# Staging slots from spent load slots, and two key gradient blocks moved behind dq, in a decode step with its gradients

## The chip, the cores and the metric

The kernel runs on one core of a Trainium2 chip. The metric is the device time of one execution in microseconds (us). The profile is of one execution on the same core; its engines are PE (TensorE matmul), PEld (TensorE weight load), DVE (VectorE), ACT (ScalarE), POOL (GpSimd) and SP (SyncE, which issues loads).

## What is computed

The reference is two rounds of a block pair, on one token for each of two batch rows, and the gradient of everything with respect to a given output gradient:

```python
def _A_ref(x, k_cache, v_cache, wq, wo):            # 32 query heads, 4 key/value heads, Sk = 16384, Dh = 128
    q = (x @ wq).reshape(B, Sq, Hq, Dh).transpose(0, 2, 1, 3)
    k, v = jnp.repeat(k_cache, rep, axis=1), jnp.repeat(v_cache, rep, axis=1)
    p = _softmax(jnp.einsum("bhqd,bhkd->bhqk", q, k) * (Dh ** -0.5), axis=-1)
    o = jnp.einsum("bhqk,bhkd->bhqd", p, v)
    return o.transpose(0, 2, 1, 3).reshape(B, Sq, Hq * Dh) @ wo

def _B_ref(x, w1, b1, w2, b2):                      # 1024 -> 3584 -> 1024
    return jnp.einsum("bsf,fd->bsd", _gelu(jnp.einsum("bsd,df->bsf", _layernorm(x), w1) + b1), w2) + b2

x = A_x
x = x + _A_ref(_layernorm(x), A_k_cache, A_v_cache, A_wq, A_wo)
x = x + _B_ref(_layernorm(x), B_w1, B_b1, B_w2, B_b2)
x = x + _A_ref(_layernorm(x), A_k_cache, A_v_cache, A_wq, A_wo)   # the same weights and caches again
x = x + _B_ref(_layernorm(x), B_w1, B_b1, B_w2, B_b2)
# returned: x, and the gradients of A_x, A_k_cache, A_v_cache, A_wq, A_wo, B_w1, B_b1, B_w2, B_b2
```

All tensors are bfloat16. The key cache, the value cache and their two gradients have 32 MB each; they are most of the 450 MB that are moved.

## The kernel before

**Order of work.** The kernel first records a list of small pieces of work (`emit`), each with the pieces of SBUF (`Chunk`) that it uses, and then `Program.run` plays the list in that order. The order within each engine is that of the list; only semaphores let engines drift apart. The stages are: attention forward, MLP forward, both again, then backward through the second MLP and attention (layer 1) and through the first (layer 0). The change concerns the end of the last stage, `attn_bwd(0, ...)`, and what stands behind it.

**Slots.** A chunk is given a slot of 1 MB (128 partitions x 4096 bfloat16). Kinds of slot: `load` (weights and cache pieces that SP loads, and a few chunks that a turned copy is written to), `full` (staging of 1 MB that a finished gradient block is cast into and stored from), `half` (staging of 0.5 MB for weight gradients). For each piece, `run` first gives slots to as many of the coming loads as it can (and thereby issues their DMA), then gives slots to the piece's own chunks, oldest free slot first, then plays the piece. A chunk's slot goes back to the list of its kind behind the piece that uses it last. A slot can be given before the store out of it has landed; the first engine that writes to it then waits for that DMA. Sixteen tiles named `slot` begin as load slots; seven of them become staging at marked steps (three `half` pairs, four `full`), and one half of the early scores tile (`e`) becomes a fifth `full` slot, the other half a load slot. Where no load is left to issue, the load slots that come free stay unused.

**The last backward pass.** It walks over eight groups (2 batch rows x 4 key/value heads), 16 blocks of 1024 keys each, in steps `s`. At a step it turns a value block on DVE (L533) and multiplies it on PE (L546), multiplies a key block of 14 steps before into the dq sum (`direct`, L571, 8 matmuls of 8 columns for a block), and takes output pieces from `outputs(s)`. For the last group it goes two blocks a step: values at steps 112 to 119, keys at 126 to 133. `N_END` is 133, the last step. Behind the steps come `dq_of` (L1048: dq of the last group, scaled and cast on DVE) and what depends on it: the rows of dq turned for the last wq gradient (`y_rows`, L1266, copied by ACT at L1267), the products of dq with wq (`tail`, 8 pieces, L461), the layernorm backward (`parts`: sums at L590, rest on DVE, and the input gradient turned by eight float32 matmuls at L613, stored by SP at L615).

**Cache gradients.** `kv_outputs(pos, g)` makes for a group 4 value and 4 key gradient blocks of 1 MB (`c` = 0 to 3). A block is one `turn` (8 transposes on PE at L1229 and a copy at L1236 or L1239) and 8 `unit`s: a 512-column matmul (L1248) into a PSUM bank and a cast of the bank into the staging slot on ACT (L272) or DVE (L275), whichever has less booked. The eighth unit has POOL issue the store (L1253). For the last group the key gradient block `c` has its units at steps `124 + 3 * c` and the one behind, its turn two steps earlier. Here they are called c0 to c3.

**Weight gradients.** `dw_units` is the same for the weights: a 512-column matmul (L1303), a cast, and a store by POOL (L1329) behind every fourth. The last 16 units, `units` in `attn_bwd`, are the wq gradient of the last key/value head, which needs dq of the last group. Five PSUM banks take the units' results in turn (`obanks`, five from step 122 on). What is left behind the last step is put in order by hand in `todo`: `kv_units` are the cache gradient pieces left, before: the last four units of c3.

Of the kernel before, what the change touches and what calls it, by code (L numbers as in the profile page):

```python
# [29 lines left out]
N_END = 133  # L30
# [27 lines left out]
class Program:  # L58


    def __init__(self):
        self.ops = []
        self.chunks = []

    def chunk(self, load=None, key=None, kind="load"):
        c = Chunk(load, key, kind)
# [41 lines left out]
    def run(self, slots):  # L108

        asked = sorted((c for c in self.chunks if c.first is not None and c.into is None and c.kind == "load"),  # L110
                       key=lambda c: c.first)
        loads = [c for c in asked if c.load is not None]
        free = {}
        for s in slots:
            free.setdefault(s[1], []).append(s)
        held = []
        nxt = 0

        def fit(c, i, among):
            fits = [s for s in among if i >= s[2] and (s[3] is None or c.last < s[3])]  # L120
            return min(fits, key=lambda s: 1 << 30 if s[3] is None else s[3], default=None)

        def possible(new, slot):

            room = [s for s in free["load"] if s is not slot]
            busy = sorted([(c.last, n, c.slot) for n, c in enumerate(held)] + [(new.last, len(held), slot)])
            n = len(held)
            for c in asked:
                if c.slot is not None or c.done or c is new:
                    continue  # L130
                if not busy:
                    return True
                while busy and busy[0][0] < c.first:
                    room.append(busy.pop(0)[2])
                s = fit(c, c.first, room)
                if s is None:
                    return False
                room.remove(s)
                n += 1
                busy.append((c.last, n, s))  # L140
                busy.sort()
                if c.first > new.last and c.first > max(h.last for h in held + [new]):
                    return True
            return True

        def give(c, s):
            free[c.kind].remove(s)
            c.slot, c.at = s, s[0]
            if c.kind == "load":
                held.append(c)  # L150
            if c.load is not None:
                c.load(c.at)

        for i, (fn, uses) in enumerate(self.ops):
            while nxt < len(loads):
                c = loads[nxt]
                s = fit(c, i, free["load"])
                if s is None or c.first > i and not possible(c, s):
                    break
                give(c, s)  # L160
                nxt += 1
            uses = [c.root() for c in uses]
            for c in uses:
                if c.slot is None:
                    s = fit(c, i, free[c.kind])
                    assert s is not None, f"piece {i}: no {c.kind} slot"
                    give(c, s)
            fn()
            for c in uses:
                if c.last == i:  # L170
                    free[c.kind].append(c.slot)
                    if c.kind == "load":
                        held.remove(c)
                        c.done = True
                    c.slot = None
# [3 lines left out]
def kernel(  # L179
# [45 lines left out]
    P = Program()  # L225
# [794 lines left out]
    def attn_bwd(l, order, gT, wo_first, outputs=None, mark=None, extra=None):  # L1020
# [9 lines left out]
        ev, wb = {}, {}  # L1030
# [45 lines left out]
        tail = []  # L1076
# [31 lines left out]
        s = 0  # L1108
# [38 lines left out]
        if l == 1:  # L1147
            todo = tail + parts
        else:
            rows, kv_units, units = outputs(s, True)  # L1150
            todo = ev.pop(s) + rows + kv_units[0:2] + tail[0:4] + kv_units[2:4] + tail[4:] + units[0:2] + parts[0:1]
            todo += units[2:4] + parts[1:2] + units[4:7] + parts[2:] + units[7:] + kv_units[4:]
        for b in todo:
            emit(*b)
        assert not ev and not wb and not pend and not extra, (ev, wb, extra)
# [29 lines left out]
    def kv_outputs(pos, g):  # L1185
# [30 lines left out]
        for c, w in [(c, w) for c in range(NCH) for w in (1, 0)]:  # L1216
            at_ = base + 4 * c + 4 * (pos == 0) if w == 1 else base + 14 + 4 * c
            if w == 0 and pos == G - 1:
                at_ = 124 + 3 * c
            stg = P.chunk(kind="full")  # L1220
            hold = {}

            def turn(c=c, w=w, hold=hold):
                st["tp"] += 1
                tp = tpb[st["tp"] % 2][:].bitcast(BF16)[:, 0:512].rearrange("p (a b) -> p a b", b=128)
                for bi in range(4):
                    for l in range(2):
                        src = d_of(l, pos, g) if w == 0 else e_of(l, g)
                        PE.transpose(tp[64 * l:64 * l + 64, bi, :],  # L1229
                                     src[:, 4 * c + bi].rearrange("p h b -> p (h b)"), ident[:])  # L1230
                st["blk"] += 1
                blk = Bt[st["blk"] % 3]
                src = tp.rearrange("p a (j t) -> p a j t", j=4)
                dst = blk[:].rearrange("p j (a t) -> p a j t", a=4)
                if st["act"] + 0.36 <= st["dve"] + 0.4:
                    S.copy(out=dst.bitcast(I32), in_=src.bitcast(I32))  # L1236
                    load_of("act", 0.36)
                else:
                    V.tensor_copy(out=dst, in_=src)  # L1239
                    dve(0.4)  # L1240
                hold["blk"] = blk

            res.append((at_ - 2, turn, ()))
            for u in range(8):
                def unit(c=c, w=w, u=u, hold=hold, stg=stg):
                    ps = ob()
                    j = u // 2
                    PE.matmul(ps, lhsT=hold["blk"][:, j, :],  # L1248
                              rhs=flat(qm(w)[:, (u % 2) * 4:(u % 2) * 4 + 4, :]), start=True, stop=True)
                    cast_out(stg.ap.rearrange("p (s j q d) -> p s q j d", j=4, q=2, d=128)[  # L1250
                        :, (u % 2) * 2:(u % 2) * 2 + 2, :, j], ps.rearrange("p (s q d) -> p s q d", q=2, d=128))
                    if u == 7:
                        GP.dma_start((dKv if w == 0 else dVv)[g, :, c * 32:(c + 1) * 32, :],  # L1253
                                     stg.ap.rearrange("p (t d) -> p t d", d=128))
                res.append((at_ + (u // 4 if pos or w == 0 else u // 3), unit, [stg, qc]))
# [323 lines left out]
    slots.append((Et[1][:, 0:CH], "load", marks["done", 0], None))  # L1579
    slots.append((Et[0][:, 0:CH], "full", marks["done", 0], None))  # L1580
    slots += [(D1t[:, j * 2048:(j + 1) * 2048], "half", marks["done", 1], None) for j in range(2)]
    P.keep(slots, lambda i: SPARE[i >= marks["e1", 1]])
    with tc.manual_schedule():
        P.run(slots)
# [30 lines left out]
```

## Time and profile before

| | before |
|---|---|
| median of 3 runs | 1114.26 us (1111.63 to 1115.72) |
| the profiled execution | 1111.95 us, span 1110.2 us |
| mean granted PE clock | 0.722 of full |
| PE / PEld / DVE / ACT / POOL busy | 74% / 55% / 69% / 44% / 16% |
| moved | 349.2 MB read, 98.6 MB written, 403 GB/s over the span |
| stores of 1 MB, from issue to landing | 14.1 us in the median |
| chain that ended last, by engine | PE 7%, DMA 6%, DVE 3% |

The span runs from the first to the last instruction of the program on the core; the execution's own time is a little longer. Busy shares are means over stages with different limits: loads and stores run almost throughout, and the engines are fuller in the last third. The row of the clock says what the throttle granted to PE; a matmul takes about twice as long at half clock. Stretches are given in us from the start of the span.

### The profile page before, as it was taken

How to read it: one execution, taken by the hardware profiler on the slowest of the kernel's cores; microseconds unless marked ns; L12 is line 12 of the kernel's file. 1: busy time of each engine (PE TensorE's matmuls, PEld its weight loads, DVE VectorE, ACT ScalarE, POOL GpSimd, SP SyncE). 2: the span in 40 equal slices, each digit the busy share in tenths (PEclk: the TensorE clock that was granted, in tenths of full speed). 3: DMA queues.
4: the chain of work that ended last, by engine and by line, in shares of the span. 5: the costliest groups of instructions: out<-in, count | busy, mean ns of one | idle time of the engine just before them, and what ended most of it. 6: DMA issues, size and time to landing. Idle time of an engine off the chain costs nothing. (4 is left out here: it accounts for less than half of the span.)

```text
span 1110.2 us, 34189 instructions
## 1 busy us (share of the span) xinstructions
PE 820.1 (74%) x14689; PEld 610.7 (55%) x14689; DVE 762.1 (69%) x1474; ACT 493.0 (44%) x1133; POOL 182.5 (16%) x577
## 2 busy tenths in 40 slices
PE   5665666457887647888778678978867986798886
PEld 4554565456777537887767564444433443344453
DVE  5864675069888637665646466978877895698874
ACT  0422223002233222245444327767766784577873
POOL 1000000001000000111111102324232332333331
PEclk9755555555555556568878658989997997699996
DMA  9999999999999998999999989999999999999994
GB/s 379 420 422 422 422 425 420 394 402 404 415 422 422 422 420 352 411 418 418 418 423 421 416 321 414 348 405 423 419 420 427 422 419 422 419 409 420 412 422 204
DMA packets 97448, 450.03 MB, mean 405 GB/s; under 512 B 7528, under 2 KB 11638, under 8 KB 58512
## 3 DMA queue, kind: packets, MB, share of 16 engines
q1 hardware_dynamic: 79504, 349.22, 77.2%
q0 software_dynamic: 17792, 98.62, 21.5%
q8 instruction: 115, 1.88, 0.6%
q14 instruction: 37, 0.30, 0.1%
HBM read 349.20 MB, written 98.62 MB: 403 GB/s over the span
## 5 line engine op out<-in xcount | busy, mean ns | idle before, releaser
L533 DVE STREAM_TRANSPOSE kT<-slot 128x512 int32<-128x512 int32 x420 | 283.4, 694 | 109.6 <-PE sc L546 86.6
L546 PE MATMUL sc<-qbd,kT 128*128 128x32 bf16 x4096 | 262.5, 222 | 11.9 <-DVE kT L533 10.4
L546 PEld LDWEIGHTS <-kT 128*128 128x128 bf16 x4096 | 209.2, 115 | 64.2 <-issue 33.3
L571 PEld LDWEIGHTS <-slot 128*128 128x128 bf16 x3520 | 144.5, 103 | 108.5 <-issue 48.1
L571 PE MATMUL sb<-xt,slot 128*128 128x8 bf16 x3520 | 161.2, 177 | 49.0 <-DMA slot<-in_A_v_cache_dram 24.4
L272 ACT CAST slot<-sc 128x512 bf16<-128x512 f32 x293 | 167.0, 593 | 64.4 <-PE sc L1303 38.9
L1248 PE MATMUL sc<-slot,late 128*128 128x512 bf16 x349 | 133.2, 404 | 17.4 <-DVE slot L275 5.4
L275 DVE CAST slot<-sc 128x512 bf16<-128x512 f32 x171 | 114.5, 678 | 30.6 <-PE sc L1248 16.2
L756 ACT ACTIVATE e<-sc 128x512 bf16<-128x512 f32 x32 | 19.0, 597 | 235.3 <-DVE sc L753 168.4
L272 ACT CAST slot<-sb 128x512 bf16<-128x512 f32 x139 | 82.5, 593 | 36.3 <-PE sb L1303 18.4
L451 ACT COPY slot<-tp 128x512 int32<-128x512 int32 x88 | 50.2, 586 | 108.6 <-PE tp L448 108.3
L448 PE MATMUL tp<-ident,slot 128*128 128x128 bf16 x768 | 72.0, 256 | 13.1 <-DMA slot<-in_A_wq_dram 7.1
L1248 PEld LDWEIGHTS <-late 128*128 128x128 bf16 x512 | 44.8, 99 | 59.5 <-issue 46.9
L581 ACT COPY xt<-e 32x128 int32<-32x128 int32 x256 | 75.6, 295 | 3.9
L1248 PE MATMUL sb<-slot,late 128*128 128x512 bf16 x163 | 66.6, 409 | 12.7 <-DVE slot L275 7.8
L1303 PE MATMUL sc<-slot,late 128*128 128x512 bf16 x160 | 64.4, 424 | 11.2 <-DVE e L275 6.2
L448 PEld LDWEIGHTS <-slot 128*128 128x128 bf16 x768 | 58.3, 117 | 15.7 <-DMA slot<-in_A_wq_dram 7.7
L433 DVE STREAM_TRANSPOSE slot<-slot 128x1024 int32<-128x1024 int32 (+1 forms) x48 | 55.3, 1178 | 16.0 <-DMA slot<-in_A_wo_dram 8.4
L275 DVE CAST slot<-sb 128x512 bf16<-128x512 f32 x81 | 54.9, 678 | 11.6 <-PE sb L1248 4.0
L638 POOL TENSOR_TENSOR m_rstd<-ln_vpe,neghalf 128x2 f32<-128x2 f32 x2 | 1.4, 716 | 349.8 <-DVE ln_vpe L636 349.8
L581 POOL COPY xt<-late 32x64 int32<-32x64 int32 x240 | 55.2, 230 | 13.0 <-DVE late L1042 1.9
L1253 POOL DMA_DIRECT2D out_dram<-slot x57 | 31.1, 546 | 157.1 <-ACT slot L272 115.2
(303 smaller groups left out, 1105.0 us busy)
## 6 DMA issues: line engine op xcount, KB each, us to landing
slot<-in_A_k_cache_dram SPq DMA_DIRECT2D x105, 1024.0 KB, 17.3
slot<-in_A_v_cache_dram SPq DMA_DIRECT2D x98, 1024.0 KB, 17.5
out_dram<-slot POOLq DMA_DIRECT2D x57, 1024.0 KB, 14.1
slot<-in_A_wq_dram SPq DMA_DIRECT2D x25, 1024.0 KB, 16.0
slot<-in_A_wo_dram SPq DMA_DIRECT2D x25, 1024.0 KB, 20.2
out_dram<-slot POOLq DMA_DIRECT2D x43, 512.0 KB, 14.2
slot<-in_B_w_dram SPq DMA_DIRECT2D x23, 896.0 KB, 15.5
slot<-in_B_w_dram SPq DMA_DIRECT2D x12, 1024.0 KB, 13.0
```

Source lines behind the costliest of these rows:

```text
L272: S.copy(out=dst, in_=src)
L275: V.tensor_copy(out=dst, in_=src)
L433: V.transpose(out=t.ap[:, h * nw * 256:(h + 1) * nw * 256].bitcast(I32).rearrange("p (w j m) -> p w j m", j=4, m=32), in_=c.ap[:, 0:4 * nc ...
L448: PE.transpose(tp[:, j * 128:(j + 1) * 128], c.ap[:, off + j * 128:off + (j + 1) * 128], ident[:])
L451: S.copy(out=d.bitcast(I32), in_=tp.bitcast(I32))
L533: V.transpose(out=kT[:].bitcast(I32).rearrange("p (w j m) -> p w j m", w=4, j=4), in_=c.ap[:, (i % 4) * 1024:(i % 4 + 1) * 1024].bitcast(I ...
L546: PE.matmul(sc[:, a0:a0 + 4, :, 2 * (i % 4) + q], lhsT=kv[:, 2 * q + w, :, e], rhs=qbd[:, q_at(g), 2 * w + e], start=(w == 0 and e == 0), ...
L571: PE.matmul(acc, lhsT=c.ap[:, n * 128:(n + 1) * 128], rhs=xv[:, i // 4, t // 2, :, 2 * (i % 4) + t % 2], start=(fresh and i == 0 and t == ...
L581: (GP.tensor_copy if on[t % len(on)] == "g" else S.copy)(out=d[32 * t:32 * t + 32, c0:c0 + cn, j, :], in_=s[32 * j:32 * j + 32, c0:c0 + cn ...
L1248: PE.matmul(ps, lhsT=hold["blk"][:, j, :], rhs=flat(qm(w)[:, (u % 2) * 4:(u % 2) * 4 + 4, :]), start=True, stop=True)
L1253: GP.dma_start((dKv if w == 0 else dVv)[g, :, c * 32:(c + 1) * 32, :], stg.ap.rearrange("p (t d) -> p t d", d=128))
L1303: PE.matmul(ps, lhsT=hold[j // 4 * 4][:, j % 4, :], rhs=Y.ap[:, y_at + c0:y_at + c0 + cn], start=True, stop=True)
```

## The change

In `run`, once every load has a slot and the piece played is past the last first use of a load-kind chunk that is not loaded (`ends`), all free load slots that have no end are put behind the free `full` slots. In `kv_outputs`, c2 and c3 of the last group get the steps `N_END + 1` and `N_END + 3` in place of 130 and 133: c2's turn falls into step 132, and c2's units, c3's turn and c3's units are left for `todo`. In `todo`, the first two of the units left stand ahead of the rows of dq, two more between the halves of the wq products as before, and the rest (c3's turn, four units of c2, eight of c3) ahead of the last seven weight gradient units instead of behind them.

```diff
@@ class Program
         self.chunks = []
+        self.ends = 0
@@ run
                 give(c, s)
                 nxt += 1
+            if nxt == len(loads) and i >= self.ends:
+                free["full"] += [s for s in free["load"] if s[3] is None]
+                free["load"] = []
             uses = [c.root() for c in uses]
@@ attn_bwd
             rows, kv_units, units = outputs(s, True)
-            todo = ev.pop(s) + rows + kv_units[0:2] + tail[0:4] + kv_units[2:4] + tail[4:] + units[0:2] + parts[0:1]
-            todo += units[2:4] + parts[1:2] + units[4:7] + parts[2:] + units[7:] + kv_units[4:]
+            todo = ev.pop(s) + kv_units[0:2] + rows + tail[0:4] + kv_units[2:4] + tail[4:] + units[0:2] + parts[0:1]
+            todo += units[2:5] + parts[1:2] + units[5:9] + parts[2:] + kv_units[4:] + units[9:]
@@ kv_outputs
             if w == 0 and pos == G - 1:
-                at_ = 124 + 3 * c
+                at_ = (124, 127, N_END + 1, N_END + 3)[c]
@@ the slots
+    P.ends = max(c.first for c in P.chunks if c.kind == "load" and c.load is None)
     P.keep(slots, lambda i: SPARE[i >= marks["e1", 1]])
```

## The prediction

> **What bounds the kernel now.** I read the page first. Its slices show an execution that the memory sets nearly to the end:
>
> ```profile
> PEclk9755555555555556568878658989997997699996
> DMA  9999999999999998999999989999999999999994
> GB/s 379 420 422 422 422 425 420 394 402 404 415 422 422 422 420 352 411 418 418 418 423 421 416 321 414 348 405 423 419 420 427 422 419 422 419 409 420 412 422 204
> ```
>
> Each column is 27.8 us. The DMA engines are full in every slice but the last, where 204 GB/s are moved. The change touches only work that stands behind key/value step 119 of the last backward pass, so only that last slice can answer. It is cut finer by the table of stretches:
>
> ```profile
> 1070.00:1080.00 10.00, 8.89 (x147) 6.13 (x143) 7.93 (x16) 7.55 (x15) 3.15 (x11) 1.00 1.02 424
> 1080.00:1090.00 10.00, 7.47 (x95) 3.79 (x92) 4.72 (x10) 3.41 (x6) 0.98 (x2) 0.67 0.81 338
> 1090.00:1100.00 10.00, 9.15 (x92) 4.92 (x90) 4.70 (x15) 4.91 (x8) 1.25 (x2) 0.50 0.34 139
> ```
>
> (busy PE, weight load, DVE, ACT, POOL, then granted clock, DMA share, GB/s). From 1080 us DMA is no longer the bound. PE is busy at a clock of 0.67 and then 0.50, DVE and ACT about half the time. The chain of waits says how that began, and the timeline what it did:
>
> ```profile
> 1062.57 0.44 PE tp L448 x8
> 1063.01 19.65 DMA out_dram<-slot
> 1082.75 0.70 DVE slot L275
> ```
>
> ```profile
> 1082.75 0.69 DVE L275 CAST slot<-sb 128x512 bf16<-128x512 f32 x1 [2.56 <-DMA out_dram<-slot]
> 1082.75 1.07 ACT L272 CAST slot<-sc 128x512 bf16<-128x512 f32 x2 [2.79 <-DMA out_dram<-slot]
> ...
> 1089.41 0.17 DVE L1048 TENSOR_SCALAR dq_all<-sb 128x8 bf16<-128x8 f32 x1
> ```
>
> Block c2 (third key gradient block of the last group) wants the staging slot whose store was issued at 1063.01 and landed 19.65 us later. Both casting engines stand still for 2.6 to 2.8 us, and PE, its five banks full, from 1081.9 to 1083.5. dq comes only at 1089.41, and the rest hangs on it. Last, the clock, in stretches of its own step (it changes at multiples of 3.41 us):
>
> ```profile
> 605.44:608.85 3.41, 3.41 (x131) 3.35 (x128) 2.20 (x4) 0.44 (x1) 0.00 (x0) 1.00 1.02 430
> 608.85:612.27 3.42, 2.57 (x60) 2.34 (x56) 3.38 (x6) 1.94 (x8) 1.77 (x8) 0.50 1.02 408
> ...
> 1073.07:1076.48 3.41, 2.30 (x43) 1.55 (x42) 2.04 (x5) 1.63 (x4) 1.08 (x2) 1.00 1.01 422
> 1076.48:1079.89 3.41, 3.41 (x66) 2.50 (x63) 2.86 (x6) 2.86 (x6) 0.00 (x0) 1.00 1.02 423
> 1079.89:1083.31 3.42, 1.94 (x32) 1.09 (x29) 0.86 (x2) 0.63 (x3) 0.53 (x1) 1.00 1.02 429
> 1083.31:1086.72 3.41, 3.23 (x44) 1.71 (x44) 2.44 (x5) 1.69 (x4) 0.45 (x1) 0.50 0.64 264
> ...
> 1096.96:1100.37 3.41, 3.41 (x13) 1.63 (x12) 2.01 (x6) 2.13 (x4) 0.72 (x1) 0.50 0.51 203
> 1100.37:1103.79 3.42, 2.35 (x9) 0.68 (x7) 3.07 (x5) 2.67 (x5) 1.46 (x2) 1.00 0.44 180
> ```
>
> The stretch with the stall (PE busy 1.94 of 3.42) is followed by half clock, and that lasts five stretches; one with 2.30 busy is not. But 605.44 shows that idleness is not needed: PE was busy throughout, with matmuls of 2, 8 and 32 columns, and the clock fell too. What counts is columns streamed. The clock came back after a stretch filled with wide matmuls (five of 512 columns, eight float32 ones of 128).
>
> **The change part by part.** The profiled execution took 1111.95 us, its span is 1110.2, so 1.75 lie around it; the median of the runs shown is 1114.26. I work out a difference of spans and take it off the median.
>
> *The pool.* At the step where the last load gets its slot (119, just behind the last value block) one load slot, that of the turned wq chunk, comes free at once; key slots follow at 121, 125, 127, 129. They queue behind the five old staging slots, oldest first, so nothing before c2 changes: c1 still takes e. c2 and c3 get former load slots with no store in flight. That removes the wait of 2.6 us. The instructions stay the same; POOL issues as many stores, and SP's queue has no load left to be passed; its one store (L615, 4 KB) now comes behind L613, well ahead of the end, with nothing behind it.
>
> *c2 and c3 behind dq.* Steps 129 to 133 lose 12 of 16 units (a 512-column matmul and its cast) and one turn; c2's turn stays in step 132. What stays is five pairs of key products at 0.57 us for 16 matmuls, and a turn of 0.41: 3.3 us. Step 129 can start at 1079.25, where PE turned c2 before. Key data is no limit: the last key load was issued at 1057.17, and landings on its tile took 20.0 us at most, so 1077.2. dq's input is thus ready at about 1082.55 instead of 1089.3, and DVE, with nothing queued, does dq at once. PE meanwhile has c2's first two units, put ahead of the row transposes; they cover the 0.87 us for which PE waited on dq before.
>
> *Behind dq.* The casts there grow from 20 to 32. Between 1079.2 and 1104.6 DVE is busy 13.14 us and ACT 11.76; some 1.4 of it is c1's. So about 23.5 us of work for two engines, 11.8 us if neither ever idled, and none of it but a 0.42 copy can start before 1082.5. At full clock (0.22 us a unit): two units 0.43, rows 0.55, half the wq products 0.83, two units 0.43, the other half 0.83, two units 0.43 end at 1086.0; the layernorm chain holds PE until 1086.9 (in before its small matmul began 1.9 us behind the products, two units in between); seven units 1.5 and the wait for DVE's seven small steps bring L613 to 1089.2, its 1.1 and c3's turn 0.41 end at 1090.8. Then 19 units are left. They go at the pace of the casts: 0.59 on ACT beside 0.68 on DVE is 0.32 a unit, as in 1100.66 to 1103.50 (nine casts in 2.84 us). 19 x 0.32 + 0.4 for a copy: last cast at 1097.3, against 1103.50.
>
> *At half clock* a unit takes 0.43, and the same list ends L613 and the turn at 1093.7 (a 0.43 + 0.55 + 0.83 + 0.86 + 0.83 + 0.86, chain to 1088.1, seven units 3.0, L613 2.0, turn 0.6). If the clock is back by 1093.5, the last cast is at 1100.3; back by 1090.1, at 1098.8; never back, 19 x 0.43 + 0.9 gives 1102.8.
>
> *The stores.* Before, the last cast to the end took 6.7 us: data until 1107.0, 3.2 us of closing. Now c2 (1 MB), c3 (1 MB) and two pieces of 0.5 MB are issued 4.8, 2.2, 1.3 and 0 us before the last cast. 3 MB at the 420 GB/s of the rows above is 7.5 us; begun 1.35 us behind c2's last cast (0.55 issue, 0.8 until bytes move, as at 1086.27), it ends 4.1 us behind the last cast instead of 3.5. So 7.3 us, not 6.7, except at half clock to the end.
>
> *Which clock.* Steps 129 to 133 become a stretch of 80 matmuls of 8 columns with a single turn in it; behind them come 64 of 2 columns among six units. By the row of 605.44 such a stretch loses the clock though PE never idles. I expect the fall in the stretch that ends near 1083 or in the next, and the return after the first or second one with seven units and L613. Ends: 1098.8 + 7.3 = 1106.1 and 1100.3 + 7.3 = 1107.6, so 4.1 or 2.6 us less than 1110.2; I take 3.4, between them.
>
> Here a page of the Trainium skill differs. "TensorE: Matmul & The Clock Gate" (Part 1, and the table in "Why this matters for your kernels") has the clock halve after an idle window of about 3.4 us and advises no idle gap over about 3 us. By that neither the 1.6 us gap of before nor the gapless list of after would lose it, and the sum would be the first rival's 1108.7; the rows of 605.44 and 1079.89 speak against it. The same page of the Trainium skill (Part 4) says that transposes do not count as busy, which would make the stretch of steps 129 to 133 thinner still; no row here separates that.
>
> **The rivals.**
>
> *The clock holds.* c2's two units, the rows' transposes and two more units follow the key products without a gap; a stretch cut at a lucky place streams as much as the one at 1073.07, which kept its clock with five wide matmuls. Then the last cast is at 1097.3 and the span 1104.6: 5.6 us less, 1108.7. For it speaks that no staging wait is left; against it 80 plus 64 thin matmuls. This is also what the idle rule of the Trainium skill gives.
>
> *Half clock to the end.* Before, five stretches passed until it returned. 1102.8 + 6.7 = 1109.5: 0.7 us less, 1113.6.
>
> *The pool does nothing.* If no load slot came free in time, c2 would take the slot of the store of 1063.01 again; that store has landed at 1082.66, when c2's first cast is now due. It would cost 0.1 us: 1110.9. The move alone dodges the stall, as the pool alone would; the two do not add.
>
> *Stores pile up at the end (slower).* 3 MB now wait on the last 5 us. If they land not as the last ones of before (3.1 to 5.1 us) but in the 14.1 us that the page has as the median for 1 MB stores, the end moves by 9 to 11 us less the 3.4 gained: about 1121. It decides once some 5 MB are queued (14.1 us at 420 GB/s is 5.9 MB); I count 3, so little speaks for it.
>
> **How the numbers follow.** Forecast: 1114.26 - 3.4 = 1110.9, chance 0.52. Clock holds 0.26, half clock 0.10, pool does nothing 0.06, piled stores 0.06. A measurement of this kernel can tell about 0.5% from no change, 5.6 us, so faster means under 1108.7. The clock-holds case lies right on it (0.15 of its 0.26 below), and the runs shown spread by 4.1 us, which puts 0.13 of the forecast's chance there too: faster 0.28. Slower is the piled stores and a little: 0.07. Same 0.65. The range runs from 1106.9 (clock holds, a run 1.8 low) to 1114.2 (half clock and 0.6 more), leaving out the piled stores and the edges.
>
> **What would show it.** Right: no wait of ACT or DVE on a store behind 1080; dq near 1082.6; c2's and c3's casts into tiles that took loads; PE without gap from 1079 to 1086; a fall of the clock between 1082 and 1087 and its return before 1094; last cast 1098 to 1101; the last 3 MB without pause. Wrong: dq later than 1084 (then the key products waited for something I did not see), a clock of 1.00 throughout (rival one), or over 8 us from last cast to end.

## The result, and the profile after

The changed kernel takes 1110.48 us in the median (17 runs, 1110.00 to 1112.35), the kernel before 1113.74 us in the same comparison (17 runs). The ratio is 0.9975, with a 95% interval from 0.9967 to 0.9982: about 2.8 us less. That is less than the 0.5% below which the prediction counts a difference as no change, though the interval does not touch 1. The forecast was 1110.9 us.

The profiled execution has a span of 1108.4 us against 1110.2. Below, line numbers of the changed kernel are 4 higher than those of before (casts L279 on DVE and L276 on ACT, units L1252 and L1307, stores L1257 and L1333, dq L1052). The page of the changed kernel, the three rows that were shown of before:

```profile
PEclk9999999997555555569868657999897998699998
DMA  9999999999999998999999989999999999999996
GB/s 372 421 422 421 422 425 421 398 404 399 418 423 421 422 421 345 409 419 421 419 423 416 417 318 411 355 399 422 420 420 425 423 419 422 420 402 421 410 423 250
```

Again only the last slice differs at the end: 250 GB/s instead of 204. (The clock differs in other slices too. That is nothing of the change: over the executions of the kernel before, its mean went from 0.71 to 0.92.) The table of stretches says what happened to the stage behind 1080 us (columns: length, busy PE, weight load, DVE, ACT, POOL, then clock, DMA share, GB/s):

```profile
1080.00:1090.00 10.00, 8.94 (x183) 6.33 (x182) 4.60 (x13) 4.87 (x9) 0.53 (x1) 0.90 0.69 286
1090.00:1100.00 10.00, 8.02 (x39) 2.78 (x37) 8.51 (x19) 7.14 (x14) 3.70 (x6) 0.92 0.64 262
```

In the second row DVE has gone from 4.70 to 8.51 us and ACT from 4.91 to 7.14, and the clock from 0.50 to 0.92: the casts are now the work, as the forecast had it. The waits behind 1075 us show that the wait on a store is gone. Each line is the waiting engine, what it waited for, and us in total, times, longest; the first lines and the longest waits of the two casting engines are:

```profile
POOL out_dram L1333 <- DVE lb_u L662: 8.6, 1, 8.6
POOL out_dram L1257 <- ACT e L276: 4.4, 1, 4.4
...
ACT slot L276 <- PE sc L1307: 2.3, 3, 1.4
ACT slot L276 <- PE sb L1252: 2.1, 1, 2.1
```

POOL's waits are a store's wait for its casts. ACT and DVE wait for PE (all but 0.5 us); the 2.8 and 2.6 us for `DMA out_dram<-slot` have no successor. In the chain of waits too (start, us, engine and line) the stretch that held 19.65 us of DMA is now work from end to end:

```profile
1080.78 1.24 PE sb L575 x48
1082.36 0.93 PE sb L575 x32
1084.28 0.89 PE sb L465 x32
1085.62 0.78 PE sb L465 x32
...
1093.57 2.96 DVE slot L279 x5
1099.56 0.76 POOLq L1615
```

The timeline shows dq, and c2's first units around it:

```profile
1083.14 0.38 PE L1252 MATMUL sb<-slot,late 128*128 128x512 bf16 x1
1083.33 0.18 DVE L1052 TENSOR_SCALAR dq_all<-sb 128x8 bf16<-128x8 f32 x1 [0.43 <-PE sb L575]
1083.36 0.38 PE L1252 MATMUL sc<-slot,late 128*128 128x512 bf16 x1
```

dq stands at 1083.33 instead of 1089.41. The clock, in stretches of its own step:

```profile
1077.86:1081.27 3.41, 3.41 (x75) 2.69 (x72) 2.83 (x5) 2.87 (x6) 0.00 (x0) 1.00 1.03 428
1081.27:1084.68 3.41, 3.41 (x98) 2.75 (x95) 1.36 (x4) 1.13 (x3) 0.53 (x1) 1.00 1.00 420
1084.68:1088.10 3.42, 2.36 (x58) 1.63 (x55) 1.84 (x6) 1.81 (x3) 0.00 (x0) 1.00 0.60 247
1088.10:1091.51 3.41, 3.41 (x11) 1.22 (x11) 2.05 (x8) 2.24 (x5) 0.72 (x1) 0.50 0.06 26
1091.51:1094.92 3.41, 3.19 (x24) 1.33 (x23) 3.06 (x7) 1.78 (x4) 0.74 (x1) 1.00 0.78 312
```

The stretch with most of the 80 eight-column products (x98) kept it; the one with the two-column products and the layernorm chain lost it; it was back after one stretch, where before it took five.

Two more things in this trace were not foreseen. The first is in the second last column of the row of 1088.10: a DMA share of 0.06 and 26 GB/s. That is one of the core's 16 DMA engines (1/16 = 0.0625) at work alone, while the 15 others have nothing. It is seen again at the very end:

```profile
1090.00:1091.00 1.00, 1.00 (x4) 0.20 (x2) 0.83 (x6) 1.00 (x3) 0.46 (x1) 0.50 0.06 25
...
1103.00:1104.00 1.00, 0.00 (x0) 0.00 (x0) 0.00 (x0) 0.00 (x0) 0.00 (x0) 0.50 1.06 434
1104.00:1105.00 1.00, 0.00 (x0) 0.00 (x0) 0.00 (x0) 0.00 (x0) 0.00 (x0) 0.50 0.29 115
1105.00:1106.00 1.00, 0.00 (x0) 0.00 (x0) 0.00 (x0) 0.00 (x0) 0.00 (x0) 0.50 0.01 4
```

Fifteen engines are done at 1104.47, the sixteenth at 1105.25. I call these 0.8 us the trail. The DMA records show how it came about. Each engine closes its part of a store with a packet of 4 bytes. For c1 fifteen of these stand by 1088.08, the sixteenth only at 1095.19, 7.1 us later. From there to 1105.24 this late engine moved its sixteenth of the last six stores (256 KB) without a pause, at 26 GB/s. The kernel before also has lone stretches, as from 1090 to 1095:

```profile
1090.00:1091.00 1.00, 1.00 (x9) 0.51 (x7) 0.00 (x0) 0.32 (x1) 0.00 (x0) 0.50 0.06 25
```

But it has no trail: its late engine had closed c3 at 1098.92, ahead of the next store's data (1099.60), and the end came from the last casts. The second is what lies behind the last data: from 1105.25 to the span's end at 1108.38 are 3.13 us, as before (1107.14 to 1110.17).

### The profile page after: what moved, and what is told of

It is laid out like the page before. It is cut to its first block, busy times and chain, and to the rows that moved or that the text cites. A ratio compares the mean times of both kernels' runs of the same rounds, so it can differ in the third digit from the quotient of the medians.

```text
span 1108.4 us, 34192 instructions
## 1 busy us (share of the span) xinstructions
PE 815.9 (74%) x14689; PEld 609.3 (55%) x14689; DVE 761.3 (69%) x1474; ACT 493.1 (44%) x1133; POOL 182.6 (16%) x577
## 3 DMA queue, kind: packets, MB, share of 16 engines
q8 instruction: 115, 1.88, 0.6%
## 5 line engine op out<-in xcount | busy, mean ns | idle before, releaser
L550 PEld LDWEIGHTS <-kT 128*128 128x128 bf16 x4096 | 209.1, 115 | 64.7 <-issue 32.9
L575 PE MATMUL sb<-xt,slot 128*128 128x8 bf16 x3520 | 161.1, 176 | 49.0 <-DMA slot<-in_A_v_cache_dram 22.9
L276 ACT CAST slot<-sc 128x512 bf16<-128x512 f32 x293 | 167.0, 592 | 60.4 <-PE sc L1307 38.0
L1252 PE MATMUL sc<-slot,late 128*128 128x512 bf16 x350 | 131.1, 397 | 17.7 <-DVE slot L279 5.7
L279 DVE CAST slot<-sc 128x512 bf16<-128x512 f32 x171 | 114.3, 677 | 27.5 <-PE sc L1252 14.2
L276 ACT CAST slot<-sb 128x512 bf16<-128x512 f32 x139 | 82.4, 593 | 37.1 <-PE sb L1307 17.0
L1252 PEld LDWEIGHTS <-late 128*128 128x128 bf16 x512 | 44.7, 98 | 62.2 <-issue 48.7
L1252 PE MATMUL sb<-slot,late 128*128 128x512 bf16 x162 | 65.6, 405 | 12.6 <-DVE slot L279 7.7
L1307 PE MATMUL sc<-slot,late 128*128 128x512 bf16 x159 | 64.0, 424 | 11.3 <-DVE e L279 6.2
L279 DVE CAST slot<-sb 128x512 bf16<-128x512 f32 x81 | 54.9, 678 | 9.7 <-PE sb L1307 4.3
L585 POOL COPY xt<-ds 32x64 int32<-32x64 int32 x128 | 29.5, 231 | 159.6 <-DVE ds L1046 104.7
```

Of the source, the lines that this page charges most:

```text
L276: S.copy(out=dst, in_=src)
L550: PE.matmul(sc[:, a0:a0 + 4, :, 2 * (i % 4) + q], lhsT=kv[:, 2 * q + w, :, e], rhs=qbd[:, q_at(g), 2 * w + e], start=(w == 0 and e == 0), ...
L575: PE.matmul(acc, lhsT=c.ap[:, n * 128:(n + 1) * 128], rhs=xv[:, i // 4, t // 2, :, 2 * (i % 4) + t % 2], start=(fresh and i == 0 and t == ...
L585: (GP.tensor_copy if on[t % len(on)] == "g" else S.copy)(out=d[32 * t:32 * t + 32, c0:c0 + cn, j, :], in_=s[32 * j:32 * j + 32, c0:c0 + cn ...
L1252: PE.matmul(ps, lhsT=hold["blk"][:, j, :], rhs=flat(qm(w)[:, (u % 2) * 4:(u % 2) * 4 + 4, :]), start=True, stop=True)
L1307: PE.matmul(ps, lhsT=hold[j // 4 * 4][:, j % 4, :], rhs=Y.ap[:, y_at + c0:y_at + c0 + cn], start=True, stop=True)
```

## The experiments

The executions differ by up to 4.6 us in the part ahead of the change (the dq of the group before the last one stands between 1074.4 and 1079.0 us). So times in the tail are counted from the start of that dq, the DVE instruction of L1048 or L1052 ahead of the last. The table has all runs, from the timeline and the DMA records of one profiled execution each; medians and ratios are of 5 to 17 runs against 17 to 35 of the kernel before on the same chip.

| run | median us | ratio to before (95%) | dq | last cast | last data | trail | span end |
|---|---|---|---|---|---|---|---|
| before | 1113.74 | 1 | 15.0 | 29.1 | 32.8 | 0 | 35.8 |
| changed | 1110.48 | 0.9975 (0.9967 to 0.9982) | 7.5 | 23.2 | 29.4 | 0.8 | 32.5 |
| e1 pool only | 1110.95 | 0.9983 (0.9972 to 0.9993) | 11.6 | 22.6 | 29.8 | 3.7 | 32.9 |
| e2 move only | 1110.83 | 0.9980 (0.9968 to 0.9993) | 7.6 | 24.8 | 30.2 | 0 | 33.3 |
| e3 wide products added | 1110.52 | 0.9983 (0.9971 to 0.9994) | 7.5 | 22.6 | 29.8 | 1.7 | 32.9 |
| e4 without c2's store | 1109.45 | 0.9969 (0.9958 to 0.9980) | 7.5 | 22.6 | 27.8 | 0 | 30.7 |
| e5 12 units left out | 1110.74 | 0.9975 (0.9965 to 0.9984) | 7.5 | 20.6 | 29.1 | 1.8 | 32.2 |
| e6 thin products added | 1112.13 | 0.9987 (0.9977 to 0.9997) | 7.5 | 23.2 | 30.4 | 1.7 (two engines) | 33.5 |
| e7 stores from SP | 1109.11 | 0.9959 (0.9946 to 0.9971) | 7.5 | 23.2 | 30.0 | 2.4 | 31.7 |
| e8 stores of 120 partitions | 1114.24 | 1.0014 (1.0002 to 1.0026) | 7.5 | 24.0 | 34.2 | – | 37.2 |
| e9 fewer PE instructions | 1111.60 | 0.9990 (0.9981 to 1.0000) | 7.5 | 24.8 | 30.2 | 0 | 33.2 |
| e10 e7 and e9 | 1110.21 | 0.9969 (0.9957 to 0.9980) | 7.5 | 23.2 | 29.2 | 1.7 | 30.9 |
| e11 e7, 120 + 8 partitions | 1110.88 | 0.9984 (0.9975 to 0.9993) | 7.5 | 24.9 | 33.1 | – | 34.5 |
| e12 before, stores from SP | 1111.20 | 0.9986 (0.9975 to 0.9998) | 15.1 | 29.1 | 32.0 | 0 | 33.5 |

### Each half of the change alone (e1, e2)

e1 keeps the three lines in `run` and has the old order:

```diff
-                at_ = (124, 127, N_END + 1, N_END + 3)[c]
+                at_ = 124 + 3 * c
```

and the two `todo` lines of before. e2 has the new order without the pool:

```diff
-            if nxt == len(loads) and i >= self.ends:
-                free["full"] += [s for s in free["load"] if s[3] is None]
-                free["load"] = []
```

> The pool rule alone; c2 and c3 at steps 130 and 133 and the order behind dq as before. Theory A (what stood in the way was the slot c2 had to wait for; the move behind dq is a second way round the same wait and costs something of its own, because c2's and c3's casts and stores then all fall on the end): the wait of 2.6 us goes, the 12 units of steps 129 to 133 keep ACT and DVE at work from about 1080 and keep wide matmuls among the thin key products, so the clock stays at 1.00; last cast about 1097, last cast to end 6.7 us as before, 6 us less than before and 2 to 3 us less than the changed kernel (about 1107.5). Theory B (the move is what gained: dq early): dq stays late, near 1086, the clock falls as before, and only the 2.6 us of the wait are gained, at most: 1111 or above, no better than the changed kernel.

> The move and the order behind dq alone, without the pool rule. c2 then takes the slot that was stored at about 1063 to 1064.5 and c3 the one stored at about 1072 to 1073. Theory A: both have landed when the first cast wants them (1083 and 1094), so it is the changed kernel again within 0.5 us: 1110.5. Rival (the prediction's count of landings is off, and the pool is what the move needs): ACT and DVE show a wait on a store again and at least 2 us of the 3.3 gained are lost: 1112.5 or above.

Each half alone takes the stall away, and each alone is worth as much as both (0.9983, 0.9980, 0.9975; the intervals lie over one another). e2 came as expected, with the clock at half for three stretches and the last cast at 24.8. It has no trail: its end came from its last casts. e1 did not. Its clock stayed at 1.00 to the end and its last cast is 0.6 us earlier than that of the changed kernel, yet it ends no earlier. The table of stretches of e1 says why:

```profile
1102.00:1103.00 1.00, 0.00 (x0) 0.00 (x0) 0.00 (x0) 0.00 (x0) 0.00 (x0) 0.91 0.98 401
1103.00:1104.00 1.00, 0.00 (x0) 0.00 (x0) 0.00 (x0) 0.00 (x0) 0.00 (x0) 0.50 0.08 29
1104.00:1106.00 2.00, 0.00 (x0) 0.00 (x0) 0.00 (x0) 0.00 (x0) 0.00 (x0) 0.50 0.07 27
1106.00:1108.00 2.00, 0.00 (x0) 0.00 (x0) 0.00 (x0) 0.00 (x0) 0.00 (x0) 0.50 0.03 10
```

Fifteen engines are done at 1103.1 us; one goes on alone to 1106.85, at 27 GB/s. What e1 won on the compute side became a trail of 3.7 us. That the two are as fast as each other is thus a coincidence of two different bounds.

e2 also says something on the clock. Its stretches around the thin products:

```profile
1080.73:1084.14 3.41, 3.35 (x95) 2.77 (x92) 0.67 (x4) 0.60 (x2) 0.53 (x1) 1.00 1.02 424
1084.14:1087.55 3.41, 3.41 (x71) 2.14 (x68) 1.45 (x3) 2.17 (x3) 0.00 (x0) 0.50 0.78 321
```

The work of this stretch is that of the changed kernel's 1081.27, which kept the clock with 98 products; here 95 products lost it with PE busy 3.35 of 3.41 us. The forecast's doubt about the idle rule of the Trainium skill ("TensorE: Matmul & The Clock Gate", Part 1) holds: by that rule a stretch with 0.06 us of idle time does not lose the clock. The row differs from the page, and the row decides.

### The clock held by added work (e3)

```diff
-  ... + units[0:2] + parts[0:1]
+  ... + units[0:2] + [(wide_, ())] + parts[0:1]     # wide_: five 512-column products, read by nobody
```

> The changed kernel plus five 512-column matmuls into a bank that nobody reads, put where PE waits 1.06 us for the layernorm sums (5 x 0.22 us fill that gap at full clock). The stretch that lost the clock (1084.7 to 1088.1) then streams about 0.6 of its time in place of 0.26. Theory A (the clock goes by columns streamed): clock 1.00 until the last cast, seven units and eight float32 turns at full clock, c2's store and the last cast 1.0 to 1.5 us earlier, the end earlier by the same: about 1109.3. Rival (the clock goes by idle time or by something else): it falls all the same, and the five matmuls cost up to 1 us: 1110.5 to 1111.5.

```profile
1079.97:1083.38 3.41, 3.35 (x97) 2.75 (x95) 1.17 (x4) 1.16 (x3) 0.53 (x1) 1.00 1.01 419
1083.38:1086.80 3.42, 3.37 (x72) 2.33 (x73) 1.86 (x7) 2.18 (x3) 0.00 (x0) 1.00 0.73 298
1086.80:1090.21 3.41, 2.58 (x15) 1.15 (x14) 2.31 (x10) 2.54 (x5) 0.72 (x1) 1.00 0.10 41
```

The first row is the stretch of the thin products, the second has the added ones. The clock held, and the last cast came 0.6 us earlier (1.0 to 1.5 were expected). That the first stretch kept it is luck: it is cut within 0.03 us of the place where e2's was, counted from the dq before, and is as busy (3.35 us), and e2 lost it there. The end did not come earlier: the trail grew from 0.8 to 1.7 us. So the lost clock of the changed kernel costs 0.6 us at the last cast and nothing at the end.

### A store left out (e4)

c2's store is not issued (1 MB of the key gradient is left out):

```diff
-                    if u == 7:
+                    if u == 7 and not (pos == G - 1 and w == 0 and c == 2):
```

> The changed kernel without the store of c2 (1 MB of the key gradient is left out). Theory A (the end is set by the 3 MB that are stored from 1095.4 on): 1 MB at 0.40 MB a us is 2.5 us, and the end comes 2 to 2.6 us earlier: about 1108. Rival (the end is set by the last cast and a fixed landing of the last store): at most 0.3 us.

The data end 1.65 us earlier than in the changed kernel, and no trail is left. Part of the forecast 2 to 2.6 us is thus there; the rest was not to be had, because with 1/16 MB less on the lone engine the other fifteen and the last cast set the end again.

### Compute left out, stores kept (e5)

This is the run that separates "the last cast sets the end" from "one DMA engine sets it". Three of the four units of each of the last four wq pieces do nothing; the stores go as before (12 of 16 units of that gradient are left out):

```diff
+                    if skip and at_ % 2048 < 1536:       # skip: the last key/value head's pieces
+                        return
                     ps = ob()[:, 0:cn]
```

> Leaves out the product and the cast of 12 of the last 16 wq gradient units (3 of each store's 4); the four stores themselves stay, with the same bytes. Compute theory (the last cast and the bytes behind it set the end): 12 casts less on ACT and DVE, the last cast about 3 us earlier, the end 2.5 to 3.5 us earlier than the changed kernel, ratio to before about 0.9945 to 0.9955. Lagging-engine theory (one of the 16 DMA engines is behind the others all through the tail and works alone at 25 GB/s at the end): the last cast also about 3 us earlier, but the data end 1 us earlier at most, and at the end a stretch of 2 us or more in which the DMA share is 0.06 and 25 GB/s; ratio about 0.997.

```profile
1102.00:1103.00 1.00, 0.00 (x0) 0.00 (x0) 0.00 (x0) 0.00 (x0) 0.00 (x0) 0.50 0.94 365
...
1104.00:1106.00 2.00, 0.00 (x0) 0.00 (x0) 0.00 (x0) 0.00 (x0) 0.00 (x0) 0.50 0.60 244
1106.00:1108.00 2.00, 0.00 (x0) 0.00 (x0) 0.00 (x0) 0.00 (x0) 0.00 (x0) 0.50 0.04 14
```

The last cast is 2.6 us earlier, the last data 0.3 us, the trail 1.8 us, the ratio 0.9975 as with all the work. Twelve casts cost nothing at the end. That is a clear verdict for the lone engine, though its stretch was a little shorter than the 2 us expected.

### Whether instruction packets make that engine late (e6, e9, e10)

The page lists 115 packets of 16 KB (1.88 MB) on a queue of its own, `q8 instruction`. They fit TensorE's instructions, 256 in a packet (the 29378 of PE and PEld are 114.8 times 256). One packet takes about 0.95 us in the trace, and in the kernel before one begins where the lone engine's series of packets ends (1098.88 to 1099.83; the series ends at 1098.92). That suggested that the late engine carries them. e6 adds 128 two-column products behind the last unit:

```diff
+                for _ in range(128):
+                    PE.matmul(tpb[0][:, 0:2], lhsT=ident[:], rhs=ident[:, 0:2], start=True, stop=True)
```

> Adds 128 two-column products (256 TensorE instructions, about one more 16 KB fetch of instructions) behind the last unit; nothing waits for them. If the engine that lags is the one that brings TensorE's instructions: one packet more on the instruction queue in the last 15 us (116 instead of 115 in all), and the engine's trail behind the others at the end 1 us longer than the 0.8 us of the changed kernel, the end 0.5 to 1.0 us later. If the lag has another cause (or the fetch falls into time in which that engine would be idle): one packet more, the trail as it was, the time within 0.3 us of the changed kernel's.

The view of the DMA queues of e6 from 1104.8 to 1105.9 us (queue: packets, MB, share), and two of its stretches:

```profile
q0 software_dynamic: 67, 0.22, 50.2%
q8 instruction: 1, 0.02, 5.5%
```

```profile
1105.00:1106.00 1.00, 0.00 (x0) 0.00 (x0) 0.00 (x0) 0.00 (x0) 0.00 (x0) 0.50 0.38 148
1106.00:1107.00 1.00, 0.00 (x0) 0.00 (x0) 0.00 (x0) 0.00 (x0) 0.00 (x0) 0.50 0.12 45
```

Packet 116 ran from 1104.87 to 1105.83, the trail grew by 0.9 us, the last data came 1.0 us later. That is the size the theory gave, but the mechanism is refuted. The row of 1106 has a share of 0.12: two engines trail, not one. In the DMA records the late engine moves its sixteen 4 KB packets of the last two stores one behind the other, 0.16 us each, from 1104.74 to 1107.25, which leaves no room for the instruction packet. A second engine carried that one: its next packet begins at 1105.81, its last ends at 1107.12. And the 1.0 us was there before packet 116 began: the late engine closed c3 27.9 us behind the dq before, against 26.9 in the changed kernel.

The last instruction packet of the changed kernel, of e1 to e5 and of e7, and the last but one of e6, show the same. While it runs (1093.75 to 1094.67 in the changed kernel), the late engine's 8 KB packets go on at 0.31 to 0.36 us each, which is 23 to 26 GB/s. With the 11 to 18 GB/s of the instruction packet on top, that would be more than any lone engine moves here (up to 27).

e9 goes the other way with the same results. In the groups at places 1 to 6 the 16 selecting products of 128 columns become 8 of 256:

```diff
-  PE.matmul(ps[:, tl, :], lhsT=sel8[...], rhs=qms["r16"][:, w, :], ...)     # 4 each, for w = 0 and 1
+  PE.matmul(ps[:, tl], lhsT=sel8[...], rhs=qms["r16"][:], ...)              # 2 each, both w at once
```

e10 is e9 with the stores of e7 (below).

> The changed kernel with fewer TensorE instructions and the same results: in the groups at places 1 to 6 the 16 selecting products of 128 columns become 8 of 256 (both w in one), 48 products and so 96 instructions less in all. In the changed kernel's trace about 31 counted TensorE instructions are left behind the last 16 KB instruction packet (1093.8 us), so with 96 less that packet should not be needed. Theory that TensorE's instruction packets ride on the lagging DMA engine and that this engine's work sets the end: 114 packets instead of 115, none behind about 1088 us, no trail of a lone engine at the end, the data end 0.8 to 1.0 us earlier (counted from the dq of the group before the last), ratio to before about 0.9966. Rival (the packets have nothing to do with the end): 114 packets, but the end within 0.3 us of the changed kernel's.

> The same saving of 96 TensorE instructions, and the last six stores from SP's queue as in the run with SP stores. If the two gains are of different parts (the lagging engine's load; what lies between the last data and the end), they add: 1.6 us for the queue and 0.8 to 1.0 us for the packet, ratio about 0.9950, and the lone engine's trail 1.4 us instead of 2.4. If they are the same time seen twice: 0.9958, as with SP stores alone.

Both have 114 packets, as forecast, the last at 1090.10 and 1087.88 us. e9 has no trail, but it proves nothing: its clock fell for three stretches, its last cast is at 24.8, and e2, with 115 packets and the same last cast, has the same end and no trail either. e10 against e7 looks better: last cast 23.2 in both, trail 1.7 instead of 2.4 us, last data and span end 0.8 us earlier. But the packet did not do this either. e10's late engine was 0.9 us ahead of e7's already when it closed the store before c1 (16.5 against 17.4 us behind the dq before), and the packet that e10 saves (1092.36 to 1093.76 in e7) ran beside the late engine's undisturbed series. e10's last three microseconds with data:

```profile
1104.00:1105.00 1.00, 0.00 (x0) 0.00 (x0) 0.00 (x0) 0.00 (x0) 0.00 (x0) 0.50 1.03 399
1105.00:1106.00 1.00, 0.00 (x0) 0.00 (x0) 0.00 (x0) 0.00 (x0) 0.00 (x0) 0.50 0.07 27
1106.00:1107.00 1.00, 0.00 (x0) 0.00 (x0) 0.00 (x0) 0.00 (x0) 0.00 (x0) 0.50 0.05 18
```

In the medians this does not show: 0.9969 for e10 against 0.9959 for e7, and 0.9990 for e9 against 0.9975 for the changed kernel. Between the 330th and the 345th MB of the loads (about 968 to 1060 us) e9 and e10 take 92.0 and 91.6 us, where the other runs take 88.6 to 91.0. Whether the wider products cost that was not followed further. In a packet's size, one trace agrees with "Runtime: NRT & Kernel Launch" of the Trainium skill ("Instruction fetch mechanics"): 256 instructions more were one packet more. The page calls the cost of such a crossing mostly hidden; no run here shows a cost of it at the end.

### The other queue, and fewer partitions (e7, e8, e11)

e7 has SP issue the last six stores (c2, c3, and the last four wq pieces):

```diff
-                        GP.dma_start((dKv if w == 0 else dVv)[g, ...
+                        (nc.sync if pos == G - 1 and w == 0 and c >= 2 else GP).dma_start((dKv if w == 0 else dVv)[g, ...
```

> The last six stores (the key gradient's third and fourth block, the wq gradient's last four pieces) are issued by SP on the hardware queue instead of POOL on the software queue. If the software queue makes one engine lag (its descriptors, or POOL's 0.6 to 0.7 us for each issue): no lone engine at the end, the data end 1 to 2 us earlier, ratio to before about 0.9960. If the lag is the engine's own (what it carries besides the stores, whichever queue): the lone stretches of 0.06 stay as they are, and the end within 0.5 us of the changed kernel's.

```profile
1103.00:1104.00 1.00, 0.00 (x0) 0.00 (x0) 0.00 (x0) 0.00 (x0) 0.00 (x0) 0.50 0.20 74
1104.00:1106.00 2.00, 0.00 (x0) 0.00 (x0) 0.00 (x0) 0.00 (x0) 0.00 (x0) 0.50 0.06 22
1106.00:1108.00 2.00, 0.00 (x0) 0.00 (x0) 0.00 (x0) 0.00 (x0) 0.00 (x0) 0.50 0.00 0
```

With 1109.11 us it is the fastest run that computes everything, and neither theory had it whole; that the first one named nearly its ratio is luck. The trail is there, on the hardware queue, and longer (2.4 us): the late engine is late whichever queue the last stores use. The last data come 0.6 us later than in the changed kernel. But from the last data (1105.70) to the span's end (1107.33) there are 1.63 us instead of 3.13. The gain is what lies behind the data, not the data. The traces show what that is. In the changed kernel POOL's closing instruction (a DRAIN at L1615, behind its last store) lasts from 1099.56 to 1107.60, 2.35 us behind the last data, and the other engines wait for it; SP was through 0.83 us behind the data. In e7, where POOL issued none of the last stores, its DRAIN is over at 1098.28, and only SP's 0.87 us are left ahead of the last 0.8 us, in which the engines wait for each other. The Trainium skill ("DMA: Bandwidth & Descriptors", "Latency and other measured facts") knows of two engines that are usually slower and guesses at the software queue's descriptor rings as the cause; here the trail stays with the last six stores off that queue. The stores ahead of them were still on it, so how the lag arose before 1087 is not told by this run.

e8 (from the changed kernel) moves only partitions 0 to 119 in these six stores, which leaves out 1/16 of them; e11 (from e7) issues c3 and the last two wq pieces as partitions 0 to 119 and 120 to 127.

```diff
-  ...dma_start(dst, src)
+  ...dma_start(dst[0:120], src[0:120])                 # e8; e11 sends 120:128 behind it
```

> The last six stores move partitions 0 to 119 only (leaves out 8 of 128 partitions of them, 0.25 MB of 4 MB). If a store's partitions go to 16 engines 8 by 8 and the lagging engine is the one of the last 8: no trail at the end, the data end 1 to 2 us earlier, ratio to before about 0.9960. If another engine lags: its trail stays at 1 to 4 us and the end stays within 0.3 us of the changed kernel's. If the 15 sixteenths land on other engines in each store: the trail is cut by what falls on it at random, the end 0.2 to 0.8 us earlier.

> The run with SP stores, its last block and its last two wq pieces each issued as partitions 0 to 119 and then 120 to 127. If 120 partitions go to 15 of the 16 DMA engines and the one left out is the lagging one: it has 0.13 MB less to move, the trail of 2.4 us at the end is gone, the end 1.5 to 2 us earlier than with whole stores. If the lagging one is among the 15: the trail stays or grows by 0.2 us, the end later by what the three more issues cost, 0 to 1 us. If stores of 120 partitions move as slowly here as on the software queue (250 instead of 400 GB/s): the end 2 us later or more.

First e8, then e11:

```profile
1102.00:1104.00 2.00, 0.00 (x0) 0.00 (x0) 0.00 (x0) 0.00 (x0) 0.00 (x0) 0.50 0.95 313
```

```profile
1102.00:1104.00 2.00, 0.00 (x0) 0.00 (x0) 0.00 (x0) 0.00 (x0) 0.00 (x0) 0.90 0.97 254
```

Both are slower, since stores of 120 partitions move at 250 to 310 GB/s with the engines as busy (0.95, 0.97) as at 400 to 430. Of e8's expectations none held; of e11's the last did. Which of the 16 engines is the late one could not be told this way, and stays open.

### The kernel before with SP's stores (e12)

> The kernel before (pool and order as they were), with its last six stores from SP's queue. If what SP's queue saves lies behind the last data (1.6 us from the data end to the span's end with SP stores against 3.1 us with the others) and has nothing to do with the change: the data end as in the kernel before (32.8 us behind the dq of the group before the last), the span's end 1.5 us earlier, ratio 0.9987, so that the change is still worth 2.5 to 3 us on top of it. If it is a gain that only the changed order has (a store's issue on POOL that held the next one): ratio 1.000. If the third block's late slot is felt more on SP, where the stores wait in one queue: ratio 1.000 or above, and c2's store later than 94.3 - 74.4 = 19.9 us behind that dq.

The edit is e7's, on the kernel before. The waits on the old slot are all there (a line of its waits):

```profile
ACT slot L272 <- DMA out_dram<-slot: 2.8, 1, 2.8
```

The data end 0.8 us earlier than before, and 1.56 us lie behind them instead of 3.03; ratio 0.9986, as expected (the 0.8 us were not). So what SP's queue saves is independent of the change: 0.9986 without it, 0.9959 with it, and 0.9975 for the change alone. The two add (0.9986 x 0.9975 = 0.9961).

## Why the prediction was right, and where it was not

The total was right: 3.4 us less forecast, 3.3 us less in the profiled tail (35.8 to 32.5), 2.8 us less by the ratio. That it came so close is partly luck, since two terms missed in opposite directions. Of its steps, these held:

- *The stall.* It goes, and pool alone or move alone removes it; "the two do not add" is what e1 and e2 show. The rival "the pool does nothing", priced at 1110.9, is e2: 1110.83.
- *dq.* 6.9 us earlier was forecast, 7.6 measured (15.0 to 7.5). The thin products ran without a gap, with the first two units of c2 behind them.
- *Which clock.* The fall was forecast in the stretch that ends near 1083 or in the next; it came in the next, which ended at 1088.10, a little later than the 1082 to 1087 that was named. The return before 1094 held (1091.51).
- *The last casts.* At full clock the sum put the last cast at 1097.3, 22.9 behind the dq before; e1, e3 and e4, with the clock held, have 22.6.

These two terms of the sum were mis-sized, and they nearly cancel:

- *The price of the lost clock.* The sum gave 1.5 to 3.0 us for one or two lost stretches. The changed kernel lost one, and its last cast is 0.6 us later than with the clock held (23.2 against 22.6). The row of 1088.10 shows why: 11 products fill PE, but DVE and ACT are busy 2.05 and 2.24 of 3.41 us and need little more from it. So the last cast came 5.9 us earlier than before (29.1 to 23.2), not the 4.0 of the middle of the forecast.
- *The stores.* "3 MB at the 420 GB/s of the rows above is 7.5 us; begun 1.35 us behind c2's last cast ..., it ends 4.1 us behind the last cast". Measured: the last data are 6.2 us behind the last cast, and the end 9.35 instead of 7.3. The prediction had named "over 8 us from last cast to end" as what would show it wrong, and in this it was. Of the 2.1 us, 0.6 are that c2's last cast came 4.2 instead of 4.8 us ahead of the last one (the 19 casts took 0.30 us each, not 0.32); 0.8 that fifteen engines needed until 1104.47, where 3.15 MB at 420 GB/s from 1.35 us behind c2's cast on would have ended at 1103.7; and 0.8 are the trail. The term took the 16 engines as one pipe of 420 GB/s. They are 16 pipes, every store lies on all of them, and one was late, by 7.1 us at c1: it worked through the quiet moments (25 GB/s from 1088 to 1091) and was still last at the end.

The first rival, "the clock holds", is refuted in its price, not only in its condition. e3 and e1 held the clock and won nothing (1110.52, 1110.95, where 1108.7 was worked out). In the changed kernel, e1, e3 and e5 the last casts lie between 20.6 and 23.2 and the last data between 29.1 and 29.8: the late engine is the floor on which all four stand. With last casts at 24.8 (e2, e9) the data end at 30.2 without a trail, so there the casts set the end again. On the compute side the change won 5.9 us at the last cast; 3.3 of them are seen at the end.

"Stores pile up" did not come: the last six stores took 5.4 us (1 MB) and 6.1 us (0.5 MB) in the median from issue to landing; the 14 us of the page are of a time in which loads fill the queues as well.

What is shown and what is not: that one DMA engine, and not the casts, sets the end of the changed kernel is shown by e5 (2.6 us less compute, 0.3 us less time), by the rows of 0.06, and by the DMA records, in which this engine has no pause from 1088 on. That TensorE's instruction packets make it late is refuted for the last of them in the changed kernel and in e1 to e7: another engine carried it. Why the lag of several microseconds was there at 1088 is not shown.

## What to carry to other kernels

When a stall near the end has two remedies that act on the same wait, expect the gain of one, and look for the next bound before pricing the second: here it was seen in the old profile, in rows where the DMA share is 0.06 and the rate 25 GB/s, which is one engine of 16 finishing alone. Price the last stores by the latest engine (what it is behind by, and a sixteenth of each store still to come at 26 GB/s), not by the sum of all. And the time behind the last data is worth a look of its own: issuing the last stores from SP instead of POOL took 1.5 us off, in the kernel before as in the changed one.

## What the runs showed of the hardware

- One of 16 DMA engines ran behind the others through the tail of nearly every run, by up to 3.7 us at the end (e1), at 25 to 27 GB/s alone. In the changed kernel it closed c1 7.1 us behind the fifteen others. Whether it is the same one in each run is not in the records.
- The last instruction packet (16 KB, 0.9 to 1.4 us) was on another engine than the late one in the changed kernel and in e1 to e7. In the changed kernel the engine that carried it closed the next store 1.4 us behind fourteen others, and was level with them again one store later.
- From the last data to the end of the span: 3.0 to 3.1 us where POOL's queue had the last stores, 1.4 to 1.6 us where SP's had (e7, e10, e11, e12). POOL's DRAIN ended 2.2 to 2.4 us behind the last data in the first, ahead of them in the second; SP was through 0.6 to 0.9 us behind the data in all.
- Stretches with stores of 120 partitions moved 250 to 310 GB/s, on POOL's queue (e8) and on SP's (e11), those of 128 some 400 to 430.
- The clock fell behind a stretch in which PE was busy 3.35 of 3.41 us with 95 products, nearly all of them 8 columns wide (e2), and held behind such stretches with 98 (the changed kernel) and 97 (e3): such a list is at the edge, and what decides was not found. Counted in columns of the products that begin in the stretch, which the prediction took for what counts, e2 and e3 are alike (some 3130 each).
